# Relu and square of an MLP's hidden tile: out of the PSUM bank, into a row of SBUF

## The chip, the core and the metric

The kernel runs on one core of a Trainium2 chip. A core has five engines that run their own instruction queues and meet at semaphores: PE (TensorE, the matmuls), DVE (VectorE), ACT (ScalarE), POOL (GpSimd) and SP (SyncE), which here issues all transfers between HBM and SBUF. PE writes its results into PSUM, which is used here as eight banks of 128 x 512 float32; DVE and ACT read and write PSUM and SBUF. The metric is the device time of one execution in microseconds, smaller is better.

## What is computed

Two blocks alternate, each twice: a gated long convolution (A) and an MLP with a squared relu (B), on 2048 tokens of width 1024, all in float32. Cut to what matters:

```python
def _A_ref(q, k, v, shift_k, ssm_k, ssm_D):
    # short causal convolution of k (4 taps), times v
    kv = k_shift * v
    # long causal convolution over all 2048 tokens, by channel, with an FFT
    y = irfft(rfft(kv) * rfft(ssm_k)) + kv * ssm_D
    return q * y

def _B_ref(x, w1, b1, w2, b2):          # w1: 1024 x 3584, w2: 3584 x 1024
    h = x @ w1 + b1
    r = jnp.where(h > 0, h, 0)
    return (r * r) @ w2 + b2

x = A_q
x = x + _A_ref(_layernorm(x), A_k, A_v, A_shift_k, A_ssm_k, A_ssm_D)
x = x + _B_ref(_layernorm(x), B_w1, B_b1, B_w2, B_b2)
x = x + _A_ref(_layernorm(x), A_k, A_v, A_shift_k, A_ssm_k, A_ssm_D)
x = x + _B_ref(_layernorm(x), B_w1, B_b1, B_w2, B_b2)
```

## The kernel before

**Units and steps.** The MLP runs as eight units, one per layer (0 or 1) and block of 512 tokens, in the order of the list `ORDER`. The first five units (0 to 4) use plain matmuls; the last three use another scheme with relus of their own (`relu_w`). A plain unit walks through the 3584 hidden features in four chunks of seven tiles of 128 features. For each tile f of a chunk, two steps of twelve matmuls accumulate `x @ w1` for 128 features and 512 tokens in one PSUM bank (tile name `p`, helper `ps1`). Two banks serve this in turn (`bufs=2`), so tile f+2 needs the bank that tile f had. Then relu, square and a split make the second layer's input, and seven steps per half of the output width accumulate `h @ w2` in four other banks. In unit 0 the last chunk's second layer works on half of the tokens at a time, with steps of six matmuls.

**The split.** Every matmul operand is kept as a pair of tiles, a rounded one (`hi`) and the rest (`lo`); a product is three matmuls: hi with hi, hi with lo, lo with hi. For the hidden tile ACT makes relu (with the bias), square and the rounded copy `rh`, and DVE subtracts to get `rl`. For the weights, SP loads a raw tile `wr`, ACT casts it to the first half of `whl`, and DVE subtracts to get the second half (line 1017). Some weights were split earlier, have been stored as pairs in HBM, and come straight into `whl`.

**What sets the order.** The program is written by one loop over all steps. Before a step's matmuls it runs the work that falls due (`lag.tick`: the hidden tile's relu one step after its last matmul, the subtraction of `rl` one step later), then moves the weights' pipeline on (`w_advance`: subtraction of the lower half for up to three steps ahead, cast for four ahead, load for eight ahead). The convolution of the other units is fed in between, by a pace per unit: transposes and small matmuls on PE, products on POOL (line 527), sums, shifted multiplies and differences on DVE (lines 531, 367, 369, 485, 486). Each engine takes its instructions in the order written. Unit 0 has no pairs to reuse for most weights, so nearly every weight is loaded raw and split there.

**Rows.** Raw weights, and some results that wait for their store, lie in a ring of eight tiles named `wr` ("rows"): `row()` hands out the next, `drop()` marks it free, and a row can be handed out again once the eighth handing-out before it has been dropped. For a weight load the loop also asks `room()`, which wants the old row dropped at least two steps ago; otherwise the load is left for a later step.

```python
def room():
    return len(ring) < RAWS or ring[-RAWS].get("freed", now[0]) < now[0] - 1

def row():
    while len(ring) >= RAWS and "freed" not in ring[-RAWS]:
        w_hi() if ptr["lo"] == ptr["hi"] else w_lo()
    x = {"t": mw.tile([P, 512], F32, name="wr", bufs=RAWS)}
    ring.append(x)
    return x
```

`relu2` is the function around the change. Its first part (k = 0) is ACT's work, its second (k = 1) DVE's. Two of the tiles of unit 1 that are made ahead use banks named `pt`, which belong to the convolution and are given back with `give`.

Of the kernel before, what the change touches and what calls it, by code (L numbers as in the profile page):

```python
# [10 lines left out]
F32 = mybir.dt.float32  # L11
F32R = mybir.dt.float32r
AF = mybir.ActivationFunctionType
# [227 lines left out]
def tile_h3_mlp(ctx: ExitStack, tc: tile.TileContext, q, kT, vT, shk, ssmT, ssmD, w1, b1, w2, b2,  # L241
                fwd_t, pro_t, inv_t, sgn_t, out):
    nc = tc.nc
    V, A, G, PE, SY = nc.vector, nc.scalar, nc.gpsimd, nc.tensor, nc.sync
# [87 lines left out]
    def give(*tiles):  # L332
        for o in tiles:
            held[slot.pop(id(o))[0]] = False
# [639 lines left out]
# [7 lines that stand above are left out]
    def drop(*xs):  # L981
        for x in xs:
            x["freed"] = now[0]
# [19 lines left out]
    def w_hi():  # L1003
        n = ptr["hi"]
        t = his[n] = mw.tile([P, 2, 512], F32R, name="whl", bufs=6)
        if from_pair(n):
            SY.dma_start(t.bitcast(F32), WD[wsrc[n]])
        else:
            A.copy(t[:, 0], raws[n]["t"])  # L1009
        ptr["hi"] += 1  # L1010

    def w_lo():
        n = ptr["lo"]
        t = wts[n] = his.pop(n)
        if not from_pair(n):
            e = WLO.get(phase[0], "V")
            ENG[e[n % len(e)]].tensor_sub(t[:, 1], raws[n]["t"], t[:, 0].bitcast(F32))  # L1017
            drop(raws.pop(n))
        ptr["lo"] += 1
# [464 lines left out]
    b1t = ml.tile([P, P], F32, name="b1t", bufs=1)  # L1484
# [1 line left out]
    lag = slag  # L1486

    def relu2(st, k):
        o = st["o"]
        if k == 0:  # L1490
            A.activation(o, o, AF.Relu, bias=b1t[:, st["f"]:st["f"] + 1])  # L1491
            A.activation(o, o, AF.Square)
            st["hi"] = ml.tile([P, T], F32R, name="rh", bufs=FC + 1)
            A.copy(st["hi"], o)  # L1494
        else:
            st["lo"] = ml.tile([P, T], F32R, name="rl", bufs=FC + 1)
            V.tensor_sub(st["lo"], o, st["hi"].bitcast(F32))  # L1497
            if st["give"]:
                give(o)

    def make_t():
        parts = [(p, dq) for p in range(FT // 2) for dq in range(2)]
# [269 lines left out]
    for s, (k, u, c, a, i, tts, w) in enumerate(steps):  # L1772
# [27 lines left out]
        if k == "m1":  # L1800
# [8 lines left out]
            o = rs[c, a]["o"]  # L1809
            for kk in range(4):  # L1810
                t = slice(kk * P, (kk + 1) * P)
                mm3(o[:, t0:t1], wh[:, t], wl[:, t], xh[:, 4 * i + kk, t0:t1], xl[:, 4 * i + kk, t0:t1],
                    i == 0 and kk == 0, i == 1 and kk == 3)
            if i == 1 and u in WINO:
                for kk in range(4 if rs[c, a]["f"] % 2 else 2):
                    lag.at(1 + kk, relu_w, rs[c, a], kk, rp)
            elif i == 1 and tts[-1] == NT - 1:
                lag.at(1, relu2, rs[c, a], 0)
                lag.at(2, relu2, rs[c, a], 1)
        elif k == "w2":  # L1820
# [6 lines left out]
            hi, lo = rp[i][a]  # L1827
            for n in range(2):
                t = slice(n * P, (n + 1) * P)
# [11 lines left out]
        else:  # L1841
            if i == 0:
                os = {tt: ps2() for tt in tts}
            r = rs[c, i]
            for tt in tts:
                t = slice(tt * P, (tt + 1) * P)
# [124 lines left out]
```

## Time and profile before

| what | value |
|---|---|
| time before, median of 3 runs | 2733.54 us (2730.44 to 2735.65) |
| the profiled execution's own time | 2727.79 us |
| its span in the profile | 2726.0 us |
| busy: PE, DVE, ACT, POOL | 2666.4, 1933.7, 1108.8, 826.1 us |
| DMA, mean over the span | 278 GB/s |
| hidden tiles that go through `relu2` | 140 (138 in banks `p`, 2 in banks `pt`) |
| units 0, and 1 to 4, in the span (about) | 130 to 520 us, 520 to 1820 us |

How the views read: a group's row gives line, engine, operation, tiles and count, then busy time and the mean of one in ns, then the time the engine was idle just before such instructions and what ended it. A row of the waits gives who waited for whom, us in total, times, and the longest. A row of the timeline gives start and duration in us, and in brackets the idle time before it. A row of a stage gives its bounds and length, then busy time and count per engine, the clock that PE was granted, the DMA share and GB/s. Matmul records overlap: PE takes one 512-wide matmul after the other at a distance shorter than a record's length.

### The profile page before, as it was taken

The page shows a single profiled execution, that of the slowest core. Times are in us where ns is not written, and L with a number is a line of the kernel's source. Part 1 is how long each engine was busy: PE and PEld are TensorE (multiplying, and loading weights), DVE is VectorE, ACT ScalarE, POOL GpSimd, SP SyncE. Part 2 cuts the span into 40 slices and gives each one's busy share as a digit, 9 for nine tenths or more (in the row PEclk, how much of TensorE's full clock was granted, in tenths as well). Part 3 has the DMA queues.
Part 4 walks back from the last instruction along what each step waited for, and adds up shares of the span by engine and source line. Part 5 has one row for each costly group of instructions (what it writes and reads, how often), then busy time and mean ns, then how long its engine had stood idle before and what let it go on. Part 6 is the DMA issues. An engine that isn't in the chain of part 4 may idle for free.

```text
span 2726.0 us, 36565 instructions
## 1 busy us (share of the span) xinstructions
PE 2666.4 (98%) x12601; PEld 2235.5 (82%) x12601; DVE 1933.7 (71%) x3070; ACT 1108.8 (41%) x1937; POOL 826.1 (30%) x531
## 2 busy tenths in 40 slices
PE   8999899899999999999999999999999999999999
PEld 7888787787888888888888888888788788888887
DVE  7878897678887777778676655366787666664565
ACT  4454344333434333342233422244355454445443
POOL 2336564255542645326453364000100010001000
PEclk9999999899999999999999999999999999999999
DMA  8889898589989898888987877688898866676556
GB/s 252 265 305 328 283 314 280 203 302 345 341 298 311 309 334 298 276 302 310 325 283 268 314 273 282 226 294 298 299 311 278 289 231 217 229 277 207 178 167 204
DMA packets 378057, 756.88 MB, mean 278 GB/s; under 512 B 43904, under 2 KB 159248, under 8 KB 377872
## 3 DMA queue, kind: packets, MB, share of 16 engines
q1 hardware_dynamic: 377872, 754.55, 81.1%
q8 instruction: 99, 1.62, 0.2%
q14 instruction: 86, 0.70, 0.1%
HBM read 604.46 MB, written 149.95 MB: 277 GB/s over the span
## 4 chain that ended last, share of the span: by engine, by line
PE 82%; DVE 8%; DMA 6%; issue 1%; ACT 1%; POOL 1%; SPq 1%; DVEq 0%; POOLq 0%; ACTq 0%
PE p L337 25%; PE p L338 25%; PE p L339 25%; PE p L1094 2%; DMA wr<-w 2%; DVE whl L1017 1%; DMA whl<-wd_m 1%; PE pt L339 1%; PE pt L337 1%; PE pt L338 1%; DMA cg<-gd 1%; DVE sm L531 1%; DVE fx L367 0%; PE pt L422 0%; PE pt L597 0%
## 5 line engine op out<-in xcount | busy, mean ns | idle before, releaser
L337 PE MATMUL p<-xh,whl 128*128 128x512 f32 (+1 forms) x1840 | 709.2, 385 | 18.8 <-DVE rl L1497 15.1
L527 POOL TENSOR_TENSOR cp<-cx,cg 128x384 f32<-128x384 f32 (+5 forms) x288 | 532.7, 1862 | 597.9 <-DVE sm L531 381.2
L338 PE MATMUL p<-xl,whl 128*128 128x512 f32 (+1 forms) x1840 | 704.4, 383 | 0.1
L339 PE MATMUL p<-xh,whl 128*128 128x512 f32 (+1 forms) x1840 | 704.1, 383 | 0.0
L1009 ACT CAST whl<-wr 128x512 fp32r<-128x512 f32 x638 | 385.4, 621 | 443.5 <-PE p L339 305.8
L1017 DVE TENSOR_TENSOR whl<-wr,whl 128x512 fp32r<-128x512 f32 x624 | 496.8, 816 | 74.3 <-ACT whl L1009 71.6
L337 PE MATMUL p<-whl,rh 128*128 128x512 f32 x1372 | 540.9, 394 | 2.8 <-DMA whl<-wd_m 2.4
L338 PE MATMUL p<-whl,rh 128*128 128x512 f32 x1372 | 536.2, 391 | 4.4 <-DVE whl L1017 4.2
L339 PE MATMUL p<-whl,rl 128*128 128x512 f32 x1372 | 535.7, 390 | 0.0
L337 PEld LDWEIGHTS p<-xh,whl 128*128 128x128 f32 x1840 | 347.2, 189 | 89.3 <-DVE rl L1497 11.7
L339 PEld LDWEIGHTS p<-xh,whl 128*128 128x128 f32 x1840 | 346.9, 189 | 67.8
L338 PEld LDWEIGHTS p<-xl,whl 128*128 128x128 f32 x1840 | 347.2, 189 | 65.6 <-DVE xl L1407 0.3
L338 PEld LDWEIGHTS p<-whl,rh 128*128 128x128 f32 x1372 | 258.7, 189 | 58.1 <-DVE whl L1017 6.5
L337 PEld LDWEIGHTS p<-whl,rh 128*128 128x128 f32 x1372 | 258.6, 189 | 57.3 <-DMA whl<-wd_m 4.6
L339 PEld LDWEIGHTS p<-whl,rl 128*128 128x128 f32 x1372 | 258.4, 188 | 54.2
L531 DVE TENSOR_REDUCE sm<-cp 128x128 f32<-128x384 f32 (+5 forms) x288 | 249.5, 874 | 16.3 <-POOL cp L527 14.0
L1595 POOL TENSOR_TENSOR acc<-acc,px 128x512 f32<-128x512 f32 x18 | 23.2, 1323 | 762.5 <-DMA px<-b 762.5
L1491 ACT ACTIVATE p<-p,b1t 128x512 f32<-128x512 f32 x138 | 91.4, 662 | 391.6 <-PE p L339 391.4
L1497 DVE TENSOR_TENSOR rl<-p,rh 128x512 fp32r<-128x512 f32 x138 | 94.8, 687 | 209.0 <-ACT rh L1494 208.8
L1559 DVE TENSOR_TENSOR rl<-wr,rh 128x256 fp32r<-128x256 f32 x84 | 49.2, 585 | 205.4 <-ACT rh L1554 205.3
L1618 DVE TENSOR_TENSOR acc<-p,acc 128x512 f32<-128x512 f32 x152 | 99.8, 686 | 86.9 <-PE p L339 86.9
L1551 ACT ACTIVATE wr<-p,b1t 128x512 f32<-128x512 f32 x84 | 57.9, 689 | 185.0 <-PE p L339 184.9
(282 smaller groups left out, 3297.5 us busy)
## 6 DMA issues: line engine op xcount, KB each, us to landing
whl<-wd_m SPq DMA_DIRECT2D x382, 512.0 KB, 5.2
wr<-w SPq DMA_DIRECT2D x494, 256.0 KB, 5.3
wr<-td SPq DMA_DIRECT2D x152, 256.0 KB, 4.2
wd_m<-whl SPq DMA_DIRECT2D x70, 512.0 KB, 6.2
cx<-xd SPq DMA_DIRECT2D x48, 512.0 KB, 5.8
cg<-gd SPq DMA_DIRECT2D x48, 512.0 KB, 6.7
gd<-fg SPq DMA_DIRECT2D x72, 256.0 KB, 6.8
cx<-xd SPq DMA_DIRECT2D x48, 384.0 KB, 5.8
```

Of the source, the lines that this page charges most:

```text
L337: PE.matmul(o, lh, rh, start=start, stop=False)
L338: PE.matmul(o, lh, rl, start=False, stop=False)
L339: PE.matmul(o, ll, rh, start=False, stop=stop)
L527: G.tensor_mul(pr.rearrange("p c i -> p i c"), xt[:, 0:j + 1], gt[:, j::-1])
L531: V.tensor_reduce(sm[:, ty, jj], st["pr"], axis=AX.X, op=OP.add)
L1009: A.copy(t[:, 0], raws[n]["t"])
L1017: ENG[e[n % len(e)]].tensor_sub(t[:, 1], raws[n]["t"], t[:, 0].bitcast(F32))
L1094: PE.matmul(o, lh, r, start=start, stop=stop)
L1491: A.activation(o, o, AF.Relu, bias=b1t[:, st["f"]:st["f"] + 1])
L1497: V.tensor_sub(st["lo"], o, st["hi"].bitcast(F32))
L1551: A.activation(r, st["o"], AF.Relu, bias=b1t[:, st["f"]:st["f"] + 1])
L1618: V.tensor_add(accs[tt][:, d], o, accs[tt][:, d])
```

## The change

Relu writes into a fresh row of the ring instead of back into the PSUM bank. Square works in the row, the rounded copy `rh` is read from the row, and the subtraction of `rl` reads the row and `rh`, both in SBUF. The bank is read by nobody after relu; a `pt` bank is given back right after relu. The row is dropped after the subtraction. The number of rows stays eight.

```diff
     def relu2(st, k):
-        o = st["o"]
         if k == 0:
-            A.activation(o, o, AF.Relu, bias=b1t[:, st["f"]:st["f"] + 1])
-            A.activation(o, o, AF.Square)
+            st["r"] = row()
+            r = st["r"]["t"]
+            A.activation(r, st["o"], AF.Relu, bias=b1t[:, st["f"]:st["f"] + 1])
+            if st["give"]:
+                give(st["o"])
+            A.activation(r, r, AF.Square)
             st["hi"] = ml.tile([P, T], F32R, name="rh", bufs=FC + 1)
-            A.copy(st["hi"], o)
+            A.copy(st["hi"], r)
         else:
             st["lo"] = ml.tile([P, T], F32R, name="rl", bufs=FC + 1)
-            V.tensor_sub(st["lo"], o, st["hi"].bitcast(F32))
-            if st["give"]:
-                give(o)
+            V.tensor_sub(st["lo"], st["r"]["t"], st["hi"].bitcast(F32))
+            drop(st["r"])
```

The order of instructions on PE and on POOL stays as it was. Two places show what becomes of the others.

DVE's queue in unit 0, last chunk, around the subtraction of `rl` for its fourth hidden tile (`p_4198` is the bank that this tile was accumulated in; `pt`, `fx`, `fg` are the convolution's). Before:

```order
L1017 TENSOR_TENSOR whl<-wr,whl 128x512
L531 TENSOR_REDUCE sm<-cp 128x128
L367 SCALAR_TENSOR_TENSOR fx<-fx,shkt 128x512 x3
L369 TENSOR_TENSOR fx<-fx 128x512
L485 TENSOR_TENSOR fg<-pt,fg 128x2x2x64
L486 TENSOR_TENSOR fg<-pt,fg 128x2x2x64
L1497 TENSOR_TENSOR rl<-p_4198,rh 128x512
L1017 TENSOR_TENSOR whl<-wr,whl 128x512
```

With the change:

```order
L1017 TENSOR_TENSOR whl<-wr,whl 128x512
L531 TENSOR_REDUCE sm<-cp 128x128
L367 SCALAR_TENSOR_TENSOR fx<-fx,shkt 128x512 x3
L369 TENSOR_TENSOR fx<-fx 128x512
L485 TENSOR_TENSOR fg<-pt,fg 128x2x2x64
L486 TENSOR_TENSOR fg<-pt,fg 128x2x2x64
L1500 TENSOR_TENSOR rl<-wr,rh 128x512
L1017 TENSOR_TENSOR whl<-wr,whl 128x512
```

The subtraction keeps its place; it reads a row now, and the bank no longer appears behind the shifted multiplies of line 367.

SP's queue in unit 0, last chunk, from the store of a convolution row (`yd`) to the stores of split second-layer weights (`wd_m`); `wr<-w` at line 1001 are the loads of raw second-layer weights. Before:

```order
L608 DMA yd_102<-wr 512x1x64
L1001 DMA wr<-w 128x512
L1025 DMA wd_m_3_0_0_4488<-whl 128x1024
L1001 DMA wr<-w 128x512 x2
L1025 DMA wd_m_3_0_2_4514<-whl 128x1024
L1001 DMA wr<-w 128x512 x3
L1025 DMA wd_m_3_0_4_4540<-whl 128x1024
L1001 DMA wr<-w 128x512
```

With the change:

```order
L608 DMA yd_102<-wr 512x1x64
L1025 DMA wd_m_3_0_0_4510<-whl 128x1024
L1001 DMA wr<-w 128x512 x3
L1025 DMA wd_m_3_0_2_4537<-whl 128x1024
L1001 DMA wr<-w 128x512 x5
L1025 DMA wd_m_3_0_4_4568<-whl 128x1024
L1001 DMA wr<-w 128x512
```

Between `yd` and the store of `wd_m_3_0_4` there were six loads and there are eight now: two weights whose loads stood ahead of `yd` are now loaded behind it, and behind one store. The rows that the relus took are the reason: the ring was not free earlier.

## The prediction

> **What bounds the kernel now.** I read the head of the page first, then PE's row in the page's groups, then PE's waits, and last the three stages in which the five plain units run.
>
> ```profile
> span 2726.0 us, 36565 instructions
> PE 2666.4 (98%) x12601; PEld 2235.5 (82%) x12601; DVE 1933.7 (71%) x3070; ACT 1108.8 (41%) x1937; POOL 826.1 (30%) x531
> ...
> L337 PE MATMUL p<-xh,whl 128*128 128x512 f32 (+1 forms) x1840 | 709.2, 385 | 18.8 <-DVE rl L1497 15.1
> ```
>
> ```profile
> PE p L337 <- DVE rl L1497: 15.1, 5, 5.1
> ...
> PE pt L422 <- DVE fx L369: 5.9, 1, 5.9
> PE p L338 <- DVE whl L1017: 4.8, 2, 4.2
> ```
>
> ```profile
> 125.00:560.00 435.00, 413.39 (x2143) 356.25 (x2144) 340.13 (x519) 186.56 (x340) 212.20 (x163) 0.97 0.85 284
> 560.00:950.00 390.00, 383.18 (x1817) 321.20 (x1816) 306.70 (x451) 152.50 (x280) 182.48 (x112) 0.99 0.92 321
> 950.00:1820.00 870.00, 866.91 (x4030) 724.55 (x4029) 587.59 (x836) 292.16 (x527) 355.00 (x191) 1.00 0.84 291
> ```
>
> PE is busy for 98% of the span, so no edit that leaves its matmuls alone can win more than the rest: 2726.0 - 2666.4 = 59.6 us, plus what slow clock costs. Of this the change can touch the first row of the waits: PE stood still five times, for 15.1 us, until DVE's `rl` had read a bank that the hidden tile's matmuls wanted. In the stages the columns are PE, PEld, DVE, ACT, POOL, granted clock, DMA share and GB/s. PE is idle for 21.6 us in the first (435.00 - 413.39), where the clock is also lowest, 6.8 in the second and 4.1 in the third. DVE is 78%, 79% and 68% busy and DMA 0.84 to 0.92: both are near enough to full that work given to them is not free by itself. The five waits in PE's timeline:
>
> ```profile
> 332.94 0.50 PE L337 MATMUL p<-xh,whl 128*128 128x512 f32 x1 [1.57 <-DVE rl L1497]
> ...
> 442.48 0.77 PE L337 MATMUL p<-xh,whl 128*128 128x512 f32 x1 [5.05 <-DVE rl L1497]
> ...
> 627.47 0.80 PE L337 MATMUL p<-xh,whl 128*128 128x512 f32 x1 [4.91 <-DVE rl L1497]
> ...
> 876.70 0.50 PE L337 MATMUL p<-xh,whl 128*128 128x512 f32 x1 [1.17 <-DVE rl L1497]
> ...
> 1302.45 0.50 PE L337 MATMUL p<-xh,whl 128*128 128x512 f32 x1 [2.34 <-DVE rl L1497]
> ```
>
> Two lie in unit 0, three in units 1 to 3. The longest shows how they come about. ACT's and DVE's timelines just before it:
>
> ```profile
> 432.02 0.66 ACT L1491 ACTIVATE p<-p,b1t 128x512 f32<-128x512 f32 x1 [2.37 <-PE p L339]
> ```
>
> ```profile
> 436.38 3.55 DVE L367 SCALAR_TENSOR_TENSOR fx<-fx,shkt 128x512 f32<-128x512 f32 x3
> 439.97 1.10 DVE L369 TENSOR_TENSOR fx<-fx 128x512 f32<-128x512 f32 x1
> ...
> 441.66 0.67 DVE L1497 TENSOR_TENSOR rl<-p,rh 128x512 fp32r<-128x512 f32 x1
> 442.25 1.46 DVE L1017 TENSOR_TENSOR whl<-wr,whl 128x512 fp32r<-128x512 f32 x1
> ```
>
> Relu was done with the bank at 432.7, nearly ten us before PE could go on. The bank was still held because `rl` stood in DVE's queue behind the shifted multiplies of the convolution, and it read the bank only at 441.66.
>
> **The change part by part. The five waits.** With the change the bank is free when Relu has read it. Relu is ACT's first work on a tile, due one step after the tile's last matmul, and PE has then one whole tile of 24 matmuls in the other bank. At the longest wait Relu's end is 442.48 - 432.68 = 9.8 us ahead of the matmul that wants the bank; the other four look alike, with several us each. So I let all five go: 1.57 + 5.05 + 4.91 + 1.17 + 2.34 = 15.0 us.
>
> **The slow clock behind two of them.** PE's timeline ahead of the longest wait, and after both long ones:
>
> ```profile
> 435.90 0.39 PE L337 MATMUL p<-xh,whl 128*128 128x512 f32 x1
> ...
> 437.03 0.39 PE L339 MATMUL p<-xh,whl 128*128 128x512 f32 x1
> ...
> 447.30 0.45 PE L339 MATMUL p<-xh,whl 128*128 128x512 f32 x1
> ...
> 631.83 0.39 PE L338 MATMUL p<-xl,whl 128*128 128x512 f32 x1
> ```
>
> Ahead of it, five intervals take 437.03 - 435.90 = 1.13 us, 0.226 each. After 442.48, eleven intervals take 4.82 us where 2.49 were due: 2.33 lost. After 627.47, ten take 4.36 where 2.26 were due: 2.10 lost. Without the waits both go, 4.4 us. Behind the wait of 2.34 us at 1302 the matmuls keep their pace, so the three short waits carry no such price. [...]
>
> **Gross gain**: 15.0 + 4.4 = 19.4 us.
>
> **What is late next.** Behind the wait at 442 the next thing that PE wants from DVE is the lower half of a weight, the row at 442.25 that ends at 443.7. It stands behind the same multiplies, and nothing in the change moves it. PE, 7.4 us earlier by wait and clock, comes to it about 1 us too early: 1.0 us comes back there (0 to 2.5). At the four other waits I found no such follower within their length.
>
> **The subtraction of `rl` reads two SBUF tiles.** The same kinds of work by form, on the two groups of units, and the weights' subtraction, which always reads two SBUF tiles, by stage (DVE, then POOL):
>
> ```profile
> L1497 DVE TENSOR_TENSOR rl<-p,rh 128x512 fp32r<-128x512 f32 x138 | 94.8, 687 | 209.0 <-ACT rh L1494 208.8
> L1491 ACT ACTIVATE p<-p,b1t 128x512 f32<-128x512 f32 x138 | 91.4, 662 | 391.6 <-PE p L339 391.4
> L1551 ACT ACTIVATE wr<-p,b1t 128x512 f32<-128x512 f32 x84 | 57.9, 689 | 185.0 <-PE p L339 184.9
> ...
> L1492 ACT ACTIVATE p<-p 128x512 f32<-128x512 f32 x138 | 80.3, 582 | 4.4
> L1552 ACT ACTIVATE wr<-wr 128x512 f32<-128x512 f32 x84 | 53.2, 633 | 2.6
> L1559 DVE TENSOR_TENSOR rl<-wr,rh 128x512 fp32r<-128x512 f32 x42 | 30.2, 718 | 139.8 <-ACT rh L1554 139.7
> ```
>
> ```profile
> 125.00:560.00 435.00, 107.77 (x110) 18.99 (x14) 0.97 0.85 284
> 560.00:1820.00 1260.00, 174.61 (x185) 0.00 (x0) 1.00 0.86 300
> 2120.00:2726.00 606.00, 141.43 (x218) 0.00 (x0) 1.00 0.66 220
> ```
>
> From the bank `rl` takes 0.687 us. From a row it takes 0.718 in the last units. The weights' subtraction takes 107.77 / 110 = 0.980 in unit 0, 174.61 / 185 = 0.944 in units 1 to 4, and 0.649 in the last stage. The stages differ in what POOL does: its adds for the convolution fill about half of the first two. So the bounds are 0.718 and 0.980, and I take the upper rows, because they are of the same units: 34 tiles x 0.293 + 106 x 0.257 = 10.0 + 27.2 = 37 us more on DVE. The cover is DVE's own idle time, 95, 83 and 282 us in the three stages; nearly all of it hides there, and where DVE is behind, as at 442, one `rl` costs 0.3 to 0.8 us. I put 1.0 us on the path (0 if it takes 0.718, up to 10.0 if all of unit 0's share shows). [...]
>
> On ACT, Relu into a row costs 689 - 662 = 27 ns more, the square 633 - 582 = 51 ns; ACT is 41% busy and Relu waits for PE (391.6 us of idle time before it), so these hide. If the cover were gone they would be 140 x 0.078 = 11 us.
>
> **The rows.** A hidden tile now takes one of the eight rows for about three steps, so raw weights are loaded later where both kinds compete: in unit 0, around the start of each second layer. By the order of the instructions, about 34 of that unit's 113 raw weights are loaded one or two steps ahead of their cast where it had been three or four. A load's price and the place where it is tightest, the last chunk (SP's timeline, with PE's matmul that needs the sixth of these weights):
>
> ```profile
> wr<-w SPq DMA_DIRECT2D x494, 256.0 KB, 5.3
> ```
>
> ```profile
> 435.67 1.34 SPq L1001 DMA_DIRECT2D wr<-w  x3
> 445.23 1.43 SPq L495 DMA_DIRECT2D gd<-fg  x3
> 446.76 0.44 SPq L1001 DMA_DIRECT2D wr<-w  x1
> ...
> 449.70 0.58 SPq L1001 DMA_DIRECT2D wr<-w  x1
> ...
> 455.48 0.34 SPq L1001 DMA_DIRECT2D wr<-w  x1
> ```
>
> ```profile
> 464.84 0.39 PE L337 MATMUL p<-whl,rh 128*128 128x512 f32 x1
> ```
>
> ```profile
> L1009 ACT CAST whl<-wr 128x512 fp32r<-128x512 f32 x638 | 385.4, 621 | 443.5 <-PE p L339 305.8 <-DMA wr<-w 58.7 <-DMA wr<-td 19.6
> ```
>
> The load at 446.76 is put back by a step or two, to between 449.7 and 452. SP cannot be sooner by much, since it holds at 445.23 for DVE's sums. Landing takes 5.3, the cast 0.62, the subtraction 0.65 to 1.46: the weight is ready between 456.3 and 459.4, and PE wants it 7.4 us earlier than before, at 457.4. So 0 to 2 us late, 1 in the middle. Four chunks have such a start, and in the first the weights are not yet tight: 3 x 1.0 = 3.0 us, with 0 below and 3 x 3 = 9 above, if a load lands as late as the last place shown (455.48) at one of them.
>
> **Sum**: 19.4 - 1.0 - 1.0 - 3.0 = 14.4 us. The profiled execution took 2727.8 us, so 2713.4 for one like it. The median of the runs shown lies 5.7 above that execution, and the runs span 5.2 us between themselves; against the median it is 2733.5 - 14.4 = **2719 us**. Its own bounds: nothing comes back, 2714; all three losses at their top (2.5 + 10 + 9 = 21.5), 2736. These need not fall together; half of their sum gives 2725.
>
> **The rivals.** *Unit 0 gives all back.* Its 8.9 us (1.57 + 5.05 + 2.33) are taken by the next waits, for loads and for DVE, since PE there depends on weights split just in time. For it speak the row of `whl` L1017 in PE's waits, 4.2 us at one place, and 21.6 us of idle PE in that stage. Against it, SP and DVE each have gaps. What stays is 4.91 + 1.17 + 2.34 + 2.1 = 10.5 of units 1 to 3, less 5 for the slower `rl`, so 2728 us.
>
> *Slower: the rows run out.* At the three tight starts of a second layer a load waits for a row that a hidden tile holds, and `rl`, which gives it back, waits in DVE's queue behind the convolution. Then each start costs a full load behind that row, 5.3 + 0.62 + 1.4 = 7.3 us, 22 us in all, and DVE's share 5 more: 19.4 - 27 = -7.5, so 2741 us. It decides from the point where the waits added in unit 0 pass 19.4 us. For it: DMA is 0.85 busy and `rl` came 10 us late at 442. Against it: after unit 0 most weights come as pairs, without a row, and the program lets a load wait only for rows dropped two steps earlier.
>
> *No change: Relu waits for its row.* The bank would then be tied to DVE as before, through the row's last reader, and the time stays at 2733.5. For it: that reader is DVE's too, a weight's subtraction or an earlier `rl`. Against it: by the order of instructions, the row was freed two steps or more earlier for about 130 of the 140 tiles.
>
> **How the numbers follow.** My forecast has 0.64, unit 0 giving all back 0.16, the slower case 0.13, no change 0.07. What a measurement of this kernel can tell from no change is about 0.2%, 5.5 us: faster is below 2728.1, slower above 2739.0. The forecast is faster but for 0.01; the first rival falls half on each side of the bound; the slower one reaches it in three cases of four. Faster 0.71, same 0.19, slower 0.10. The range goes from 2711 (no loss, and 3 us for the scatter of the medians) to 2734, which takes in the first and the last rival and leaves out the slower one and a little of the forecast's tails.
>
> **What would show it.** Right: the row of waits for `rl` L1497 is gone from PE's waits, and none for Relu has come; no slow matmuls after about 435 and 622; the clock of the first stage goes from 0.97 to 0.98 or more; `rl` takes 0.9 to 1.0 us before 1820 us; PE's idle time in the three stages falls by 5, 5 and 3 us or so. Wrong: PE waits of some us for `whl` L1017 or for a load at the starts of the second layer in unit 0; Relu with idle time ended by DVE or by a store instead of PE; a longer POOL add. I would be wrong altogether if unit 0 took as long as before, or longer, with its five waits gone.

## The result and the profile after

The change takes 2720.18 us (median of 4 runs, 2718.25 to 2721.39) beside 2734.60 us of the kernel before: a ratio of 0.9947, 95% interval 0.993 to 0.9965. Run again later beside the experiments it gave 2720.33 us (5 runs) and 0.994 (0.9926 to 0.9954). That is 14.4 us won, the forecast's 14.4 to the digit. That the two agree to the digit is luck: the two executions that were profiled differ by only 2727.79 - 2719.04 = 8.75 us, and the parts of the sum are not where I put them.

The head of the page of the changed kernel, and its row of the hidden tiles' matmuls:

```profile
span 2717.3 us, 36601 instructions
...
PE 2663.3 (98%) x12601; PEld 2232.8 (82%) x12601; DVE 1989.9 (73%) x3070; ACT 1125.3 (41%) x1937; POOL 844.3 (31%) x531
...
L337 PE MATMUL p<-xh,whl 128*128 128x512 f32 (+1 forms) x1840 | 707.0, 384 | 3.6 <-DMA whl<-wd_m 3.6
```

PE's waits after the change:

```profile
...
PE p L337 <- DMA whl<-wd_m: 9.0, 13, 1.4
PE pt L422 <- DVE fx L369: 8.0, 3, 6.7
PE p L338 <- DVE whl L1017: 4.3, 4, 3.1
...
PE pt L597 <- DVE fg L486: 2.6, 1, 2.6
...
PE p L337 <- ACT whl L1009: 1.0, 1, 1.0
```

The row for `rl`, 15.1 us before, is gone, and none for Relu has come. In its place stand a wait for `fg` that was not there, 2.1 us more for `fx` (5.9 before) and 5.1 us more for the stored pairs `wd_m` (3.9 before). DVE is busy 56 us more. The stages (PE, PEld, DVE, ACT, POOL, clock, DMA share, GB/s), and the two groups that the change rewrote:

```profile
125.00:560.00 435.00, 413.02 (x2141) 354.74 (x2142) 351.17 (x520) 190.71 (x339) 217.86 (x163) 0.98 0.85 284
560.00:950.00 390.00, 388.49 (x1857) 326.51 (x1856) 334.25 (x460) 156.98 (x282) 190.14 (x114) 1.00 0.94 327
950.00:1820.00 870.00, 869.03 (x4039) 726.47 (x4038) 612.94 (x850) 304.99 (x535) 360.07 (x190) 1.00 0.84 291
```

```profile
L1500 DVE TENSOR_TENSOR rl<-wr,rh 128x512 fp32r<-128x512 f32 x140 | 144.0, 1029 | 183.8 <-ACT rh L1497 183.7
L1492 ACT ACTIVATE wr<-p,b1t 128x512 f32<-128x512 f32 x138 | 95.2, 690 | 368.8 <-PE p L339 367.9 <-DVE rl L1500 0.9
```

PE's idle time fell by 5.3 us in the second stage and by 2.1 in the third (3.1 before), and not at all in the first (21.6 before, 22.0 now). Relu still waits for PE, 367.9 of its 368.8 us, and for a row only 0.9 us. So the rows don't hold Relu. In this profile unit 0 gave back all it won.

Since PE's order is the same in all kernels here, the same matmul can be looked up in each trace. Three such marks in PE's timeline, before and after: the first matmul of unit 0, the first transposes behind unit 0, and the 7489th matmul of lines 337 to 339, about the end of unit 4:

```profile
124.39 0.36 PE L337 MATMUL p<-xh,whl 128*128 128x256 f32 x1
...
526.86 1.97 PE L1704 MATMUL p<-ident,wr 128*128 128x128 f32 x8 [3.84 <-DVE wr L1695]
...
1834.38 0.39 PE L337 MATMUL p<-whl,rh 128*128 128x512 f32 x1
```

```profile
124.51 0.36 PE L337 MATMUL p<-xh,whl 128*128 128x256 f32 x1
...
526.25 1.97 PE L1706 MATMUL p<-ident,wr 128*128 128x128 f32 x8 [3.83 <-DVE wr L1697]
...
1824.96 0.39 PE L337 MATMUL p<-whl,rh 128*128 128x512 f32 x1
```

The differences of the marks, for one profiled execution of each kernel, in us (the labels are those of the experiments below):

| kernel | unit 0 | units 1 to 4 | rest of the span | median of its runs |
|---|---|---|---|---|
| before | 402.5 | 1307.5 | 891.6 | 2734.6 |
| before, second (`again`) | 401.5 | 1313.8 | 890.7 | 2735.3 |
| the change | 401.7 | 1298.7 | 892.3 | 2720.2 |
| the change, second (`after2`) | 404.1 | 1301.1 | 891.2 | 2720.3 |
| `u14` | 401.4 | 1300.9 | 892.0 | 2720.0 |
| `u0` | 405.5 | 1312.4 | 892.8 | 2735.3 |
| `hold` | 408.1 | 1316.5 | 894.5 | 2745.0 |
| `yt0` | 399.5 | 1299.7 | 890.0 | 2714.4 |
| `yt0b` | 400.9 | 1299.0 | 890.9 | 2716.9 |
| `yt0l3` | 401.8 | 1298.5 | 890.4 | 2716.3 |
| `pool0` | 409.7 | 1299.1 | 891.0 | 2721.3 |
| `ytpool0` | 407.8 | 1297.7 | 890.0 | 2722.2 |
| `dve0` | 419.2 | 1298.0 | 893.8 | 2734.2 |
| `dve14` | 401.8 | 1322.3 | 891.1 | 2743.3 |

Where one kernel stands twice, or two are alike in a part, they differ by up to 4 us in unit 0 and 6 in units 1 to 4; that is the grain of a single execution.

### The profile page after: what moved, and what is told of

It is laid out like the page before. It is cut to its first block, busy times and chain, and to the rows that moved or that the text cites. A ratio compares the mean times of both kernels' runs of the same rounds, so it can differ in the third digit from the quotient of the medians.

```text
span 2717.3 us, 36601 instructions
## 1 busy us (share of the span) xinstructions
PE 2663.3 (98%) x12601; PEld 2232.8 (82%) x12601; DVE 1989.9 (73%) x3070; ACT 1125.3 (41%) x1937; POOL 844.3 (31%) x531
## 4 chain that ended last, share of the span: by engine, by line
PE 81%; DMA 8%; DVE 5%; POOL 2%; issue 2%; ACT 1%; SPq 1%; DVEq 0%; POOLq 0%; ACTq 0%
PE p L338 24%; PE p L337 24%; PE p L339 24%; PE p L1094 2%; DMA whl<-wd_m 2%; DVE whl L1017 1%; DMA wr<-w 1%; PE pt L338 1%; PE pt L337 1%; PE pt L339 1%; DMA cg<-gd 1%; DMA wd_m<-whl 1%; DMA fg<-ssmT 1%; POOL cp L527 1%; DMA cx<-xd 0%
## 5 line engine op out<-in xcount | busy, mean ns | idle before, releaser
L527 POOL TENSOR_TENSOR cp<-cx,cg 128x384 f32<-128x384 f32 (+5 forms) x288 | 543.7, 1901 | 565.3 <-DVE sm L531 360.0
L1500 DVE TENSOR_TENSOR rl<-wr,rh 128x512 fp32r<-128x512 f32 x140 | 144.0, 1029 | 183.8 <-ACT rh L1497 183.7
L1492 ACT ACTIVATE wr<-p,b1t 128x512 f32<-128x512 f32 x138 | 95.2, 690 | 368.8 <-PE p L339 367.9
L1553 ACT ACTIVATE wr<-p,b1t 128x512 f32<-128x512 f32 x84 | 57.9, 689 | 186.7 <-PE p L339 186.7
```

What stands on the lines that cost most here:

```text
L527: G.tensor_mul(pr.rearrange("p c i -> p i c"), xt[:, 0:j + 1], gt[:, j::-1])
L1492: A.activation(r, st["o"], AF.Relu, bias=b1t[:, st["f"]:st["f"] + 1])
L1500: V.tensor_sub(st["lo"], st["r"]["t"], st["hi"].bitcast(F32))
L1553: A.activation(r, st["o"], AF.Relu, bias=b1t[:, st["f"]:st["f"] + 1])
```

## Experiments

**The kernel before, again.** No edit.

> The kernel before, unchanged, to see how far its own runs lie apart and what differs between them. Theory: the five waits for the subtraction of rl are always there, and the slow clock behind two of them varies from run to run, so a second profile shows the same five places, within 1 us each, and another length of the slow stretch; ratio 1.000 +- 0.001. Rival: the five waits themselves come and go between executions, so that the profile shows other places or a sum other than 15 us by more than 3 us.

2735.31 us (11 runs, 2728.26 to 2737.44), ratio 0.9992 (0.9982 to 1.0003). The rival held in part: the five places stay, and the sum is 3.1 us larger. The trace has seven waits for `rl`, the same five and two more:

```profile
PE p L337 <- DVE rl L1497: 18.2, 7, 4.7
```

The place that matters is in unit 1. In the first profile PE hardly waited there; in the second it stood for 4.04 us and ran at about half its pace behind it. PE first, the first profile's row and then the second's two:

```profile
720.32 0.47 PE L337 MATMUL p<-xh,whl 128*128 128x512 f32 x1 [0.74 <-ACT p L1491]
```

```profile
724.75 0.77 PE L337 MATMUL p<-xh,whl 128*128 128x512 f32 x1 [4.04 <-DVE rl L1497]
...
727.44 0.55 PE L337 MATMUL p<-xh,whl 128*128 128x512 f32 x1
```

The six intervals from 724.75 to 727.44 took 2.69 us where 1.36 were due. What differs lies on DVE and POOL. DVE's shifted multiplies ahead of `rl`, and POOL's work beside them, first profile:

```profile
717.25 2.33 DVE L367 SCALAR_TENSOR_TENSOR fx<-fx,shkt 128x512 f32<-128x512 f32 x3 [0.16 <-ACT fx L364]
```

```profile
715.47 1.35 POOL L677 TENSOR_TENSOR sm<-sm 128x512 f32<-128x512 f32 x1 [2.81 <-ACT p L1492]
718.94 2.05 POOL L527 TENSOR_TENSOR cp<-cx,cg 128x640 f32<-128x640 f32 x1 [2.13 <-DMA cg<-gd]
```

and second:

```profile
719.67 4.33 DVE L367 SCALAR_TENSOR_TENSOR fx<-fx,shkt 128x512 f32<-128x512 f32 x3
```

```profile
718.13 1.34 POOL L677 TENSOR_TENSOR sm<-sm 128x512 f32<-128x512 f32 x1 [2.82 <-DVE sm L531]
719.43 1.77 POOL L527 TENSOR_TENSOR cp<-cx,cg 128x640 f32<-128x640 f32 x1
721.15 1.17 POOL L681 TENSOR_TENSOR sm<-sm 128x256 f32<-128x256 f32 x1
722.40 1.05 POOL L682 TENSOR_TENSOR sm<-sm 128x256 f32<-128x256 f32 x1
```

In the first, POOL stood idle for 2.13 us for a load, and three multiplies took 2.33 us. In the second the load had come, POOL worked on to 723.45, and the same three, from 719.67 to 724.00, took 4.33. One pair of executions would not show that POOL is the reason; all of the first trace does. Of its 72 multiplies of line 367, taken one by one, the 32 that met POOL at work for at most a twentieth of their time took 0.70 to 0.75 us, and the 7 that met it for all but a twentieth took 1.10 to 2.19. So here, with the bank held until DVE reads it, PE's time hangs on whether POOL happens to work (0.74 or 4.04 us of waiting at this place). The second profile also shows a slow stretch behind the wait of 2.34 us that had none in the first:

```profile
1308.38 0.80 PE L337 MATMUL p<-xh,whl 128*128 128x512 f32 x1 [2.34 <-DVE rl L1497]
...
1311.11 0.56 PE L337 MATMUL p<-xh,whl 128*128 128x512 f32 x1
```

Six intervals, 2.73 us: 1.37 lost. The kernel before had 28 runs beside the first four experiments, from 2729.05 to 2741.10, 12 us apart; the change had 9, from 2717.22 to 2722.36, 5 us apart. The execution profiled for the prediction (2727.79) was faster than any of these 28.

**The bank held as before, all else changed.**

```diff
             V.tensor_sub(st["lo"], st["r"]["t"], st["hi"].bitcast(F32))
             drop(st["r"])
+            V.tensor_copy(ml.tile([P, 1], F32, name="hx", bufs=2), st["o"][:, 0:1])
```

(A `pt` bank is given back behind the copy, too.)

> The change, with the bank's release undone: after the subtraction of rl DVE copies one column of the bank, so the bank is held as long as before; rows, reading SBUF and all else stay. Theory (the gain is the earlier release): the five waits come back, now for this copy, and the costs of the change stay, so 2735 to 2742 us, no faster than before. Rival (rows in SBUF themselves pay, since fewer instructions read PSUM): about 2720 us as with the change.

2745.00 us, ratio 1.0035 (1.0025 to 1.0046). The waits are back, now for the copy:

```profile
PE p L337 <- DVE hx L1500: 13.2, 6, 4.8
```

```profile
L1500 DVE COPY hx<-p 128x1 f32<-128x1 f32 x138 | 20.5, 148 | 0.0
```

This row does not have all of them. At the six matmuls that waited in one or both profiles of before, PE waits again in `hold`, for 2.81, 4.84, 4.89, 3.72, 1.30 and 2.47 us, 20.0 in all, and for nothing at any of them in the change's trace; the profile puts three of the six down to another releaser than the copy. So the gain is the release of the bank; without it the row and the slower subtraction cost 8.7 us against the kernel before (2736.33 beside these runs), 3 above what I expected at most. That is an upper bound for them, since the copies add 20.5 us to DVE. The release in turn is worth at most 2745.0 - 2720.2 = 24.8 us. At the prices per microsecond of DVE that the doubling below gives, 0.61 in unit 0 (a fifth of the copies) and 0.18 behind it, an estimate for the copies is 2.5 + 3.0 = 5.5 us, so the loss of the release and not the copies is the larger part.

**The change in units 1 to 4 alone, and in unit 0 alone.** The old `relu2` serves the other units; here and below a hidden tile's record also carries the number of its unit, `u`:

```diff
+    def relu2(st, k):
+        (relu2_new if st.get("u", 0) > 0 else relu2_old)(st, k)     # u14; u0: == 0
```

> The change in units 1 to 4 only; unit 0 keeps relu in its bank. Theory one (by the two profiles unit 0 gives back all it wins, 0.3 to 0.7 us are left): 2718 to 2722 us, the same as the whole change. Theory two (as predicted, about half of unit 0's 8.9 us stays): 2724 to 2727 us.

> The change in unit 0 only. Theory one (unit 0 gives back all): 2733 to 2735 us, no difference from before; PE's two waits for rl in unit 0 gone, others come for the convolution's sums and the weights of the second layer. Theory two: 2729 to 2731 us.

`u14`: 2719.97 us, ratio 0.9943 (0.9931 to 0.9956). `u0`: 2735.34 us, ratio 0.9994 (0.9981 to 1.0007). Theory one, both times. In `u14` two waits for `rl` are left, unit 0's, and cost nothing in the end; in `u0` they are gone from unit 0 and the convolution and the second layer's weights have taken their place:

```profile
PE p L337 <- DVE rl L1497: 7.0, 2, 5.4
```

```profile
PE pt L422 <- DVE fx L369: 8.8, 5, 5.0
...
PE pt L597 <- DVE fg L486: 2.5, 1, 2.5
PE p L337 <- ACT whl L1009: 2.3, 1, 2.3
```

How unit 0 gives it back stands in the changed kernel's trace, most of it around the wait of 5.05 us at 442.48 that is gone. DVE, then PE:

```profile
431.97 1.50 DVE L1500 TENSOR_TENSOR rl<-wr,rh 128x512 fp32r<-128x512 f32 x1
...
438.27 3.58 DVE L367 SCALAR_TENSOR_TENSOR fx<-fx,shkt 128x512 f32<-128x512 f32 x3
...
443.24 0.41 DVE L486 TENSOR_TENSOR fg<-pt,fg 128x256 f32<-128x256 f32 x1
```

```profile
260.34 0.72 PE L422 MATMUL pt<-ident,fx 128*128 128x128 f32 x4 [1.13 <-DVE fx L369]
...
438.31 0.39 PE L337 MATMUL p<-xh,whl 128*128 128x512 f32 x1
...
443.80 2.04 PE L597 MATMUL pt<-sm,yh 128*128 128x128 f32 x8 [2.60 <-DVE fg L486]
...
463.64 0.50 PE L337 MATMUL p<-whl,rh 128*128 128x512 f32 x1 [0.98 <-ACT whl L1009]
...
478.76 0.50 PE L337 MATMUL p<-whl,rh 128*128 128x512 f32 x1 [1.42 <-DMA whl<-wd_m]
```

The loss begins ahead of both waits that unit 0 had: at 260.34 PE stands for the convolution's DVE work, where it did not stand before, and by 300 us it is 2.5 us behind the old trace, matmul by matmul. The matmul that waited until 442.48 now runs at 438.31. But DVE is late as well: `rl` starts at 431.97 and takes 1.50 us (429.87 and 0.69 before), and the multiplies begin at 438.27, 1.9 us later than before (436.38). A dozen matmuls on, PE wants a bank of the convolution that DVE's line 486 has yet to read, and stands for 2.60 us. Both waits come with the change in unit 0: the ten kernels that free unit 0's banks early all have them, for 0.4 to 5.0 us at the first place and 1.5 to 4.9 at the second; the four that don't (before, `again`, `u14`, `hold`) wait at most 0.2 us at the first and not at all at the second. Then come the sixth weight and the stored pairs. PE is 6.5 us ahead of the old trace just before the wait for line 486, and 2.4 when its matmuls have their pace again behind it; at the sixth weight it is 1.2 ahead (464.84 and 463.64), and at the pairs 1.7 behind.

**Unit 0 without the rows.** Its hidden tiles go through two tiles of their own, `yt`, which lie idle in this unit:

```diff
-            st["r"] = row()
+            st["r"] = {"t": ml.tile([P, 512], F32, name="yt", bufs=2)} if st.get("u", 0) == 0 else row()
```

> The whole change, but unit 0's hidden tiles go through two tiles of their own (a name that lies idle in unit 0), so that the ring of eight rows is left to the raw weights there. Theory one (what unit 0 loses is lost to late weight loads): the waits for the sixth weight of the last second layer and for the pairs stored from it, 4 to 5 us, are gone, 2715 to 2717 us. Theory two (it is lost on DVE, whose subtraction takes 1.03 us in place of 0.69, and to the convolution behind it): those waits may go, but PE only comes earlier to DVE's next work, 2719 to 2721 us as with the change.

2714.38 us (4 runs, 2713.73 to 2722.45), ratio 0.9941 (0.992 to 0.9962): by the median theory one, by the interval open. Once more, with the change itself on the same chip:

> Unit 0's hidden tiles in two tiles of their own, unchanged from before, now beside the change: if the rows cost 4 to 5 us in unit 0, 2714 to 2717 us and its interval below that of the change; if the first runs were chance, 2718 to 2722 us.

> The change itself, unchanged, beside the others on one chip: 2718 to 2722 us, ratio 0.994 to 0.996.

2716.89 us (0.9926, 0.9914 to 0.9939) beside 2720.33 (0.994, 0.9926 to 0.9954). The intervals overlap; over all nine runs of each the medians are 2716.4 and 2720.3, and six of the nine with `yt` lie below every run of the change. So by these runs the rows cost some 3 to 4 us, and this is the best of the versions, if by little. The waits that theory one names went in part only: the one for the cast of the sixth weight fell from 1.0 us (the change; 0.6 in `after2`) to nothing in `yt0` and 0.3 in `yt0b`, while those for the stored pairs stayed in unit 0, 1.7 and 2.8 us with the rows, 2.1 and 1.9 without. SP's load of the sixth raw weight in the last chunk, with the change and in `yt0b`:

```profile
457.16 2.86 SPq L1001 DMA_DIRECT2D wr<-w  x3
```

```profile
449.89 0.44 SPq L1001 DMA_DIRECT2D wr<-w  x1
```

Before, this load went at 446.76. With the change it goes at 457.16 (the first of the three in this row), behind a store, since the ring had no free row for it earlier; with the rows left to the weights it goes at 449.89.

**Unit 0's subtraction on POOL.** In the changed kernel, and with the two tiles of `yt0`:

```diff
-            V.tensor_sub(st["lo"], st["r"]["t"], st["hi"].bitcast(F32))
+            (G if st.get("u", 0) == 0 else V).tensor_sub(st["lo"], st["r"]["t"], st["hi"].bitcast(F32))
```

> The whole change, but unit 0's subtraction of rl (about 34) is done by POOL instead of DVE, rows from the ring. Theory (DVE bounds unit 0): DVE has some 35 us less to do there, PE's waits for fx and fg fall by 3 to 6 us, 2714 to 2718 us. Rival (DVE and POOL share what bounds unit 0): POOL's 34 x 1.36 us more delay its products, which DVE then waits for, 2720 to 2727 us.

> Both of the former: unit 0's hidden tiles in two tiles of their own, their subtraction on POOL. If both losses are real and apart, 2711 to 2715 us, the best of all; if POOL is what unit 0 waits for, 2720 to 2727 us, and since only two such tiles stand, Relu waits for POOL's subtraction and PE for Relu.

2721.25 us (0.9953, 0.9941 to 0.9964) and 2722.17 us (0.9963, 0.995 to 0.9976): the rival. Unit 0 took 409.7 and 407.8 us in the two profiles, 6 to 8 more than with DVE; by the medians `pool0` loses 1 us against the change (its profiled execution, 2726.01, was 4.8 above its median) and `ytpool0` 5.7 against the nine runs with `yt`. PE's waits of `pool0`:

```profile
PE pt L422 <- DVE fx L369: 12.4, 4, 8.8
...
PE pt L597 <- DVE fg L486: 3.8, 1, 3.8
```

DVE has less to do there, and PE waits longer for it. DVE in turn waits longer for POOL's products, as the rival has it: in unit 0, 19.2 us in `pool0` beside 10.2 with the change, and 15.0 in `ytpool0` beside 7.8 in `yt0b`. Here nothing was won by giving this work to POOL.

**DVE's work, doubled.** The subtraction done twice, in unit 0 (on top of `yt0`), and in units 1 to 4 (on top of the change):

```diff
             V.tensor_sub(st["lo"], st["r"]["t"], st["hi"].bitcast(F32))
+            if st.get("u", 0) == 0:                           # dve14: > 0
+                V.tensor_sub(st["lo"], st["r"]["t"], st["hi"].bitcast(F32))
```

> As the former, and unit 0's subtraction of rl is done twice on DVE, the second writing the same again (about 35 us more work in unit 0, none in what PE computes). Theory (what is left of unit 0's loss is DVE's): 10 to 20 us slower than without, 2725 to 2735 us, with PE's waits for fx and fg grown. Rival (DVE's work hides, as the prediction had it, a tenth of it on the path): 2717 to 2720 us.

> The change, with the subtraction of rl done twice on DVE in units 1 to 4 (the second writes the same again; some 115 us more work there, none for PE). Theory (in these units DVE's work hides, since PE no longer waits for it there and most weights come as pairs; only unit 0 pays for it): 2719 to 2726 us. Rival (DVE's work shows everywhere at the rate of unit 0, half of it on the path): about 2775 us.

2734.21 us (0.9998, 0.9989 to 1.0007) and 2743.31 us (1.0031, 1.0017 to 1.0045). The added instructions in the two stages (DVE busy, count, clock, DMA share, GB/s), of `dve0` and of `dve14`:

```profile
125.00:520.00 395.00, 30.20 (x28) 0.97 0.86 288
```

```profile
520.00:1820.00 1300.00, 120.93 (x111) 0.99 0.83 291
```

In unit 0, 30.2 us cost 419.2 - 400.7 (the mean of the three kernels with `yt`) = 18.5 us: six tenths lie on the path, and PE's waits for `fx` and `fg` grew as expected, from 8.2 and 1.5 us in `yt0b` to 14.5 and 4.9. In units 1 to 4, 120.9 us cost 1322.3 - 1300.2 (the mean of the change, `after2` and `u14`) = 22.1 us: 0.18, between the theory and its rival. The medians say about the same, 17.3 us (against `yt0b`) and 23.0 (against the change). My theory that DVE's work hides there altogether falls.

**One step later.** As `yt0b`, with unit 0's subtraction of `rl` due three steps behind the tile instead of two:

```diff
-                lag.at(2, relu2, rs[c, a], 1)
+                lag.at(2 if u else 3, relu2, rs[c, a], 1)
```

> As yt0b, but unit 0's subtraction of rl is issued one step later, which the bank no longer hinders: the same work on DVE behind the convolution's instead of ahead of it. If the order on DVE sets what PE waits for in unit 0, 2 to 4 us faster than yt0b, 2711 to 2714 us; if it is the sum of DVE's work, the same as yt0b, within 1.5 us.

2716.30 us (0.9927, 0.9915 to 0.9939): the same as `yt0b`. This bit of DVE's order does not count there; that the sum of its work does is what `dve0` shows.

## Why the prediction was right, and where it was wrong

**The five waits (15.0 us): right, and too few.** All went, since Relu ends well ahead, and `hold` shows that the release is what does it. But the profile was of an execution in which a sixth wait, at 720, took 0.74 us; in the second it took 4.04. Two profiles of the kernel before would have shown 15.1 and 18.2 us.

**The slow clock (4.4 us): right in kind.** That the short waits carry no such price was wrong: the wait of 2.34 us at 1302 cost nothing in one execution and 1.37 us in another, and the one at 720 brought 1.33 of its own (by the distance of the matmuls, about 0.45 us in both places where 0.226 was their pace). In the first profile's trace the granted clock was 1.00 from 434.90 to 437.03, ahead of the longest wait, 0.50 behind it (442.48 to 447.30), 0.51 behind the wait at 627 (627.47 to 631.83), and 1.00 behind the one at 1302 (1302.45 to 1305.00). So one kernel paid differently in two executions for the same wait of 2.34 us; what decides it no run here shows.

**What is late next (1.0 us, 0 to 2.5): the step that failed in unit 0.** I looked for the weight's lower half. The next thing PE wanted from DVE was the convolution's bank behind line 486, and its row stood in the old trace too, just ahead of `rl`:

```profile
441.33 0.41 DVE L486 TENSOR_TENSOR fg<-pt,fg 128x256 f32<-128x256 f32 x1
```

There PE's lead went from 6.5 us to 2.4, so 4.1 us came back by the two traces, above the bound: 2.6 us of standing still, the rest matmuls at slow clock (granted 0.55 from 443.80 to 447.00). And 2.4 us more were lost to the convolution's `fx` by 300 us, ahead of both waits, where I had looked for nothing.

**`rl` from SBUF (1.0 us on the path): the duration near, the path wrong.** The subtraction by stage, before and after:

```profile
125.00:520.00 395.00, 19.13 (x28) 0.97 0.90 300
520.00:1820.00 1300.00, 77.06 (x112) 0.99 0.85 295
```

```profile
125.00:520.00 395.00, 25.48 (x28) 0.98 0.90 300
520.00:1820.00 1300.00, 118.54 (x112) 1.00 0.85 297
```

0.683 became 0.910 us in unit 0 (28 tiles, not the 34 that I counted up to 560 us), 0.688 became 1.058 in units 1 to 4; I had 0.980 and 0.944. (POOL's work in these stages, which I called adds, is for the most part the products of line 527.) That is 6.4 and 41.5 us more for DVE. I let nearly all of it hide under DVE's idle time. At the prices of the doubling, 0.61 and 0.18, an estimate of what it costs is 3.9 and 7.5 us. The second is too high if work hides better the less there is of it: from the second profile of before, units 1 to 4 had some 17.4 us to win (12.6 of waits, 2.1 + 1.33 + 1.37 of slow clock, the 2.1 from the first profile) and won 12.7 to 15.1, so 2.3 to 4.7 went there. The mean share of busy time, 78%, misled me: DVE waits at some places and is late at others.

**The rows (3.0 us, 0 to 9): right in size, as far as the scatter lets one say.** By `yt0b` beside the change 3.4 us, by the marks in unit 0 about 2.6 (403.3, the mean of the change, `after2`, `u0` and `dve14`, against 400.7), which is within the grain of single executions. The load that I let go back to 452 at the latest went at 457.16.

**The sum.** I had 4.6 of the 14.4 us in unit 0 and 9.8 behind it, if the 1.0 us for `rl` is shared out by tiles. (PE's idle time in the third stage was 870.00 - 866.91 = 3.1 us, not the 4.1 that I wrote; no term hung on it.) Measured it is nothing that can be told from zero in unit 0 (by `u0` 1.0 us won, the interval from 5 won to 2 lost; by `u14` beside the change 0.2), and in units 1 to 4 all, 8.8 us against the first profile and 15.1 against the second. Two errors cancel, which is luck: unit 0 gave back what I thought it would keep, and units 1 to 4 win more than that profile could show. The first rival's mechanism, *unit 0 gives all back*, is what happened there; its 2728 us was wrong by the same hidden wait. If the kernel before always ran as in its first profile, that rival would have been the nearer one: 2727.8 - 5.5 = 2722 us, where the forecast's sum gives 2713 and 2720 was measured.

**The other rivals.** *The rows run out*: in the changed kernel's unit 0 the new waits took about what had been won and no more, far from the 22 us of this rival. *Relu waits for its row*: 0.9 us in all.

What stays open: how the 3.9 us of DVE, the rows and the bank behind line 486 share out in unit 0, since they fall on the same places, and whether a version with more rows for all would keep `yt0`'s gain; none was run.

## To carry to other kernels

When a buffer is given back by an engine that has other work in its queue, give it back with the first engine that has read it; the gain is in the wait as it is in a usual execution, so look at more than one profile before pricing it, above all where one engine's work takes longer while another is at work, as DVE's three multiplies did here (2.33 and 4.33 us). Then ask what the waiting engine wants next from the same late engine, and read that off the trace at the place, since nothing in such a change brings the late engine earlier. A share of idle time on the late engine need not cover more work on it: double a piece of its work and see what share of it the end moves by, stage by stage (0.61 and 0.18 here).

## What the runs showed that I had not expected

An execution luckier than the median hid most of a stall (0.74 us of waiting where the second had 4.04): three multiplies took 2.33 or 4.33 us, by whether POOL was waiting for a load at that time. The subtraction of `rl` came to depend on POOL's work as well, with one input in PSUM before and both in SBUF after (shortest, median and longest of one, in ns):

```profile
L1497 DVE TENSOR_TENSOR rl<-p,rh x138: 673/691/693, 143.6 to 1806.6; 128x512 fp32r<-128x512 f32 x138
```

```profile
L1500 DVE TENSOR_TENSOR rl<-wr,rh x140: 673/693/2917, 143.8 to 1797.3; 128x512 fp32r<-128x512 f32 x140
```

The median does not move; the long ones are those that meet POOL. In the trace of the change, 34 ran while POOL was at work for all but a twentieth of their time, with a mean of 1.53 us, and 74 that met it for at most a twentieth took 0.69, none over 0.695. Before, 41 met POOL at work for all but a twentieth, and none took over 0.693. Why DVE's work takes longer beside POOL's no run here shows. Whether POOL pays too is not settled: the mean of its 288 products (line 527) is 1862 and 1861 ns in two profiles of before and 1901 and 1906 in two of the change, but 1875 in `hold`, whose `rl` reads SBUF as well.

The price of a microsecond of DVE differed by a factor of three between stages in which DVE is busy for 82% and 75% of the time: 0.61 in unit 0 and 0.18 in units 1 to 4. And the nine runs of the change lie within 5 us, where 28 of before lay within 12, which no term of my sum spoke of; that the change makes the time steadier is not shown, since nine runs are few, and the nine with `yt` lie 11 us apart.
